# First batch of a dilated sliding-window attention with a SiLU layer behind it: v in two halves, a new order of steps, copies assigned later in the plan, band mask by a scan

## The chip, the cores and the metric

The kernel runs on one core of a Trainium2 chip. It is timed as a whole, in device microseconds; a figure is the median of several executions. The core has five engines with instruction queues of their own: TensorE (PE in the profile; its weight loads are PEld), VectorE (DVE), ScalarE (ACT), GpSimd (POOL) and SyncE (SP). Each engine works through its queue strictly in the order in which the program was written; engines wait for each other through semaphores. Transfers from and to HBM are started by an instruction on POOL, SP or ACT and are then carried out by 16 DMA engines.

## The reference

Attention over 8 batches, 8 heads, 576 positions, head size 64. Heads 0 to 3 look back over 32 positions, heads 4 to 7 over every fourth of the last 128. The result, 4608 tokens by 512, passes through two dense layers.

```python
mask_plain = (rel >= 0) & (rel < window)                       # window 32
mask_dil = (rel >= 0) & (rel < window * dilation) & (rel % dilation == 0)   # dilation 4
masks = np.stack([mask_plain if h < H // 2 else mask_dil for h in range(H)], axis=0)
scores = np.where(masks[None], scale * np.matmul(q, k.transpose(0, 1, 3, 2)), -1000000000.0)
attn = softmax(scores)                                         # over the last axis
x = np.matmul(attn, v).transpose(0, 2, 1, 3).reshape(B * S, H * D)
h = x @ w_in                                                   # 512 x 2048
g = h * (1.0 / (1.0 + np.exp(-h)))
out = g @ w_out                                                # 2048 x 512
```

## The kernel before

Layer 1 and layer 2 work on ten groups of tokens, two of 256 and eight of 512. Layer 1 (`layer1`, from line 849) makes 16 tiles h of 128 columns of the hidden layer by four matmuls each; ScalarE takes the tanh (th), VectorE makes gT of it. Layer 2 (`layer2`) sums 16 matmuls into a y tile; ScalarE copies it to ob and sends it out.

Attention (`attention`) is written per batch as steps with names. TD, TA and TB transpose k and q on PE, and a copy brings them from PSUM to kqD (dilated heads), kP and qP (plain heads). S makes one set of scores and exp gives probs; V copies v of the dilated heads to vd; P and D are the value matmuls of the plain and dilated heads, with a reciprocal and a product on VectorE behind each; XP and XD transpose the result into xA, from which layer 1 reads. Batches 0 to 2 go this way; from batch 3 on k and q are turned by DMA through DRAM (kq_s), two batches ahead.

Batch 0 is special. Its k and q arrive in two parts: rows 0 to 95 (k) and rows 0 to 95 (q) of a tile first, and the remaining 48 rows of both later, as load `k0`. TR and TS transpose that rest. Its masks are added in PSUM, by a matmul of the identity with mask_d or mask_p (line 594), and turned into factors once batch 0 is over (step M, line 638). The masks come from `band`, a 128 x 128 matrix with ones where 0 <= column - row < 32, which POOL makes with a memset and two selects (lines 195 to 200).

The order of everything is made by a planner when the program is built (classes `Step` and `Plan` from line 258 on and the loop at the end). `Plan` keeps a time for PE, times at which ScalarE and VectorE are free, and the times at which PSUM buffers come free; costs in us stand with each `yield`. The loop takes the first step among the next 8 of attention, the next of layer 1 and the next of layer 2 whose inputs are due. Due times of loads are constants: the list `ORDER` is the order of the loads on POOL behind the first ones, `LOAD_US` how long each takes, and `AT_DIL`, `AT_PLAIN`, `AT_VRAW`, `AT_VP` when the first ones land. No time of the planner is seen by the chip: what the program holds is one fixed order per engine.

Where a copy may run on either engine, `best` compares the two engines' free times and gives one. It does so at the moment at which the copy is handed to the planner's queue, with a bias `LEAN` toward ScalarE for batch 0.

POOL's loads use eight semaphores in turn, so that a load is not issued before the load eight places earlier has landed. For v of the plain heads a batch has 24 blocks of 128 rows (4 heads, 6 positions j), 96 rows apart. In batch 0 block 0 of head 0 starts before the tensor and is built from `v_head` (SP, line 190); the other 23 are one load (line 177).

Of the kernel before, what the change touches and what calls it, by code (L numbers as in the profile page):

```python
# [16 lines left out]
def kernel(  # L17
# [18 lines left out]
    MR = M - MA  # L36
    QB = P - W
# [17 lines left out]
    ORDER = "k0 r0 w0a w0b w1 w2 w3 d1 p1 r1 o0 v1 o1 o2 o3".split()  # L55
    LOAD_US = {"w": 2.6, "o": 2.6, "d": 3.7, "p": 3.7, "r": 1.4, "v": 2.6, "k0": 2.0, "r0": 0.9, "w0a": 1.3, "w0b": 1.3}
    AT_W0 = 12.6
# [12 lines left out]
    ident = cpool.tile([P, P], F16, name="ident")  # L70
# [35 lines left out]
    def nat_of(b, key):  # L106
        i = ("k", "q", "rest").index(key)
        return nats[b % 2][:MA, i * RW : (i + 1) * RW].rearrange("p (h r d) -> p h r d", h=H, r=DIL)
# [67 lines left out]
    def issue_vp_first():  # L176
        nc.gpsimd.dma_start(out=vps[0][:, 1:, :D], in_=v_win(QB - W, HN * NB - 1, QB * D))  # L177

    v_head = xRs[2][:, 0, : 2 * D].bitcast(F32)
    for t in vraws[::-1]:  # L180
        nc.vector.memset(t, 0.0)
    nc.vector.memset(v_head[:W], 0.0)
    nc.vector.memset(kqDs[0][:, :, :, 0, MA:], 0.0)
# [6 lines left out]
    nc.sync.dma_start(out=v_head[W:], in_=v[0, 0, :QB])  # L190
# [4 lines left out]
    nc.gpsimd.memset(band, 1.0)  # L195
    for s, base in ((1, 0), (-1, W - 1)):
        nc.gpsimd.affine_select(
            out=band, in_=band, compare_op=ALU.is_ge, fill=0.0, base=base,
            pattern=[[s, P]], channel_multiplier=-s,
        )  # L200
    issue_vp_first()
    nc.vector.tensor_copy(vps[0][:, 0, :D], v_head)
# [4 lines left out]
    nc.vector.memset(mask_p[:W, :2], -BIG)  # L207
    for t in probs:
        c = 2 * 4 * MH
        n = PW + P - c  # L210
        nc.scalar.copy(t[:, c:], vraws[1].rearrange("p a h r d -> p (a h r d)")[:, :n])
# [5 lines left out]
    for what in ORDER:  # L217
        kind, n = what[0], int(what[1])
        if kind == "w":
            f0, f1 = {"": (0, 4), "a": (0, 2), "b": (2, 4)}[what[2:]]  # L220
            cols = slice((4 * n + f0) * P, (4 * n + f1) * P)
            nc.gpsimd.dma_start(out=w_in16[:, :, cols], in_=wi[:, :, cols])
        elif kind == "o":
            nc.gpsimd.dma_start(  # L224
                out=w_out16[:, 4 * n : 4 * n + 4], in_=wo[:, 4 * n : 4 * n + 4]
            )
        elif what == "k0":
            issue_part(k, MA, M, nat_of(0, "rest"), 0, H)
            issue_part(q, MA, M, nat_of(0, "rest")[MR:], 0, H)
        elif what == "r0":  # L230
            issue_vraw(0, (1,))
        elif kind == "d":
            issue_nat(n, HN, H)
        elif kind == "p":
            issue_nat(n, 0, HN)
        elif kind == "r":
            issue_vraw(n)
        else:
            issue_vp(n)
        at += LOAD_US[what] if what in LOAD_US else LOAD_US[kind]  # L240
        AT[what] = at
        if kind == "w":
            for f in range(f0, f1):
                AT_WIN[4 * n + f] = at
# [11 lines left out]
    LEAN = 0.3  # L256
# [6 lines left out]
    class Plan:  # L263
        def __init__(self):
            self.t = 0.0
            self.now = 0.0
            self.free = {"ACT": 0.0, "DVE": 0.0}
            self.heap = []
            self.n = 0
            self.rings = {nm: [] for nm in RINGS}  # L270

        def push(self, step, gen, ready):
            self.now = ready
            try:
                eng, us = next(gen)
            except StopIteration:
                step.done = ready
                return
            heapq.heappush(self.heap, (ready, self.n, step, gen, eng, us))
            self.n += 1  # L280

        def flush(self):
            while self.heap and self.heap[0][0] <= self.t:
# [5 lines left out]
                if eng == "LANDED":  # L289
                    self.push(step, gen, ready)  # L290
                    continue
                end = max(ready, self.free[eng]) + us
                self.free[eng] = end
                self.push(step, gen, end + HOP)
# [36 lines left out]
    AT_DIL = {0: 6.3, 1: AT["d1"], 2: t2 + 7.0}  # L331
    AT_PLAIN = {0: 9.5, 1: AT["p1"], 2: t2 + 7.0}
    AT_VRAW = {0: 10.4, 1: AT["r1"], 2: t2 + 8.6}
    AT_VP = {0: 12.9, 1: AT["v1"], 2: t2 + 11.4}
    AT_CAST = t2 + 18.0
    AT_REST = AT["k0"]
    AT_V1 = AT["r0"]
    AT_WOUT = [AT[f"o{n}"] for n in range(4)]
# [96 lines left out]
    def attention(b):  # L435
# [46 lines left out]
        def best(dve, act):  # L482
            ends = {
                e: max(plan.now, plan.free[e]) + us for e, us in (("DVE", dve), ("ACT", act))
            }
            return ("DVE", dve) if ends["DVE"] + LEAN * (b == 0) <= ends["ACT"] else ("ACT", act)

        def trans_a(ring, hp):
# [6 lines left out]
            for dst, src, us in (  # L495
# [4 lines left out]
                step = best(us, us)  # L500
                yield step
                copy_on(step[0], dst, src.rearrange("p r m -> p m r"))

        def trans_b(ring, hp):
# [3 lines left out]
            step = best(0.47, 0.40)  # L508
            yield step
            qt = qP[:, hp].rearrange("p (m r) -> p m r", r=DIL)  # L510
            copy_on(step[0], qt[:, MR:], tps.rearrange("p r m -> p m r"))

        def trans_d(ring, h):
            tps = small(ring, [P, 2, 3, MA], F16, f"td_{b}_{h}")
            for rp in range(2):
# [5 lines left out]
            step = best(0.37, 0.58)  # L521
            yield step
            copy_on(
                step[0], kqD[:, h].rearrange("p r k m -> p r (k m)"),
# [3 lines left out]
        def trans_d0(ring, h):  # L528
# [6 lines left out]
            step = best(0.34, 0.42)  # L535
            yield step
            copy_on(step[0], kqD[:, h].rearrange("p r k m -> p (r k) m")[:, :, :MA], tps)

        def trans_d1(ring):
            tps = small(ring, [P, 2 * HN, MA], F16, f"td1_{b}")  # L540
            for n in range(2 * HN):
                nc.tensor.transpose(
                    tps[:, n],
                    nat_of(b, "rest")[:, HN + n // 2, n % 2 * 2 : n % 2 * 2 + 2, :], ident[:MA, :MA],
                )
            step = best(0.60, 0.72)
            yield step
            copy_on(
                step[0], kqD.rearrange("p h r k m -> p (h r k) m")[:, :, MA:],
                tps.rearrange("p n (k m) -> p (n k) m", k=2),  # L550
            )

        def trans_a0(ring, hp, nm):
# [7 lines left out]
            step = best(0.47, 0.42)  # L561
            yield step
            dst = (kP[:, hp, W:] if nm == "k" else qP[:, hp])[:, : DIL * MA]
            copy_on(step[0], dst.rearrange("p (m r) -> p m r", r=DIL), tps.rearrange("p r m -> p m r"))

        def trans_a1(ring, hp):
            tps = small(ring, [P, DIL, MA], F16, f"ta1_{b}_{hp}")
            for r in range(DIL):
                for i in range(2):
                    nc.tensor.transpose(  # L570
                        tps[i * D : i * D + D, r], nat_of(b, "rest")[:, 2 * hp + i, r, :],
                        ident[:MA, :MA],
                    )
            for n, dst in enumerate((kP[:, hp, W:], qP[:, hp])):
                step = best(0.27, 0.22)
                yield step
                copy_on(
                    step[0], dst[:, DIL * MA :].rearrange("p (m r) -> p m r", r=DIL),
                    tps[:, :, n * MR : n * MR + MR].rearrange("p r m -> p m r"),
# [46 lines left out]
        def paired(key):  # L626
            step = best(0.335, 0.95)
            yield step
            src = nat_of(b, key)
            copy_on(  # L630
                step[0], pairs[key].rearrange("p g r i d -> p i g r d"),
# [8 lines left out]
        def vd_of(ab):  # L640
            step = best(0.335, 0.95) if pe_path else ("DVE", 0.335)
            yield step
            copy_on(step[0], vd[:, ab, :, :, :D], vraws[b % NV][:, ab])
# [48 lines left out]
        def x_p(ring, j):  # L692
# [6 lines left out]
            step = best(0.17, 0.22)  # L699
            yield step  # L700
            copy_on(step[0], dst, xp)

        def x_d(ring, ab):
# [8 lines left out]
            for hp in range(HP // 2):  # L712
                step = best(0.365, 0.36)
                yield step
                copy_on(step[0], dst[:, hp], xp[:, hp].rearrange("p r m -> p m r"))

        if b == 0:
            order = [
                ("TD", 0), ("TD", 1), ("TD", 2), ("TD", 3), ("S", 3), ("S", 4), ("TA", 0, "k"),
                ("TA", 1, "k"), ("TA", 0, "q"), ("TA", 1, "q"), ("V", 0), ("D", 0, 0), ("D", 0, 1),  # L720
                ("S", 0), ("D", 0, 2), ("S", 1), ("D", 0, 3), ("XD", 0), ("P", 0), ("P", 1), ("P", 2),
                ("XP", 0), ("XP", 1), ("XP", 2), ("TR",), ("TS", 0), ("TS", 1), ("S", 5), ("P", 3),
                ("S", 2), ("V", 1), ("S", 6), ("XP", 3), ("P", 4), ("P", 5), ("D", 1, 0), ("D", 1, 1),
                ("XP", 4), ("XP", 5), ("D", 1, 2), ("D", 1, 3), ("XD", 1), ("M",), ("B",),
# [26 lines left out]
        for key in order:  # L751
# [31 lines left out]
            elif kind == "S":  # L783
                if not pe_path:
                    deps = [turned[b]]
                elif b == 0:
                    deps = [st for key_, st in steps.items() if key_[0] == "TA" and a[0] < 3]
                    deps += [st for key_, st in steps.items() if key_[0] == "TS" and a[0] == 2]
                    deps += [st for key_, st in steps.items() if key_[0] == "TD" and a[0] > 2]
                    deps += [st for key_, st in steps.items() if key_[0] == "TR" and a[0] > 4]  # L790
                elif a[0] < 3:
                    deps = [steps[t, hp] for t in ("TA", "TB") for hp in range(HP // 2)]
                else:
# [3 lines left out]
                    deps + readers.get(base + a[0] - NP, []), ("ACT", "DVE"),  # L797
# [3 lines left out]
            elif kind == "P":  # L801
# [3 lines left out]
                    [at_vp] + [steps["S", u] for u in us], ("DVE",),  # L805
# [131 lines left out]
    while att or l1 or l2:  # L937
# [13 lines left out]
        cands = main + cands if side > 0.5 else cands + main  # L951
        pick, waits = None, []
# [47 lines left out]
```

## Time and profile before

| | us |
|---|---|
| median of 5 runs | 318.32 |
| lowest, highest | 317.58, 321.53 |
| profiled execution, whole | 318.8 |
| its span (first to last instruction) | 317.1 |
| PE busy in the span | 302.9 |
| VectorE busy | 194.7 |
| ScalarE busy | 165.3 |
| POOL busy | 53.5 |

The span is what the instructions cover; the rest of the execution's 318.8 us lies around it. Busy time is the union of an engine's instructions. A matmul's row includes the time that its result takes through the array, so rows of neighbouring matmuls overlap and a busy PE is not always at its peak rate.

How the start goes by in the timeline:

| us | what |
|---|---|
| 5.2 | PE's first transpose (TD), when the first k has landed |
| 6.3 | VectorE scales the band, when POOL has made it |
| 7.8 | first mask matmul of the scores |
| 11.6 | first value matmuls (D) |
| 15.7 | TR, on the rest of k and q |
| 21.2 | first matmuls of layer 1 |
| 32.6 | first transposes of batch 1 |
| 40.1 | first matmuls of layer 2 |
| 58.1 | first transposes of batch 2 |
| 313.2 | last ob |

### The profile page before, as it was taken

Reading aid. Unit: us, or ns where it says so; the run is one execution under the profiler, and the core shown is the slowest. Engines: PE = TensorE matmul, PEld = TensorE weight load, DVE = VectorE, ACT = ScalarE, POOL = GpSimd, SP = SyncE. Lnnn points to the kernel's source line nnn. Section 1 sums busy time; section 2 is a strip of 40 time slices with the busy share of each in tenths; the row PEclk is TensorE's granted clock in tenths of the full one; section 3 lists DMA queues with packets and bytes.
Section 4 is the critical chain, followed back from the end, with each engine's and each line's share of the span. In section 5 each row is a group of like instructions: output and inputs, shape, how many; then the busy total and the mean of one; then the engine's idle time right before and its main releaser. Section 6 shows DMA issues by size and latency. Waiting matters only on the chain.

```text
span 317.1 us, 6091 instructions
## 1 busy us (share of the span) xinstructions
PE 302.9 (96%) x2378; PEld 155.0 (49%) x2378; DVE 194.7 (61%) x489; ACT 165.3 (52%) x306; POOL 53.5 (17%) x85
## 2 busy tenths in 40 slices
PE   2999898999999999999999999999999999999995
PEld 1567774545544544544454444444454444444442
DVE  5448997699788785853777578538773155555000
ACT  7668774477766365444663455446642344555111
POOL 8734814001900005001400050000000000000000
PEclk9999999999999999999999999999999999999999
DMA  7999999998999949998999999990114600000221
GB/s 96 179 203 196 175 201 180 218 174 140 126 199 203 201 99 159 214 189 192 163 180 193 207 158 207 177 219 24 53 54 124 179 2 33 33 33 2 84 81 66
DMA packets 107124, 44.50 MB, mean 140 GB/s; under 512 B 73304, under 2 KB 102488, under 8 KB 107096
## 3 DMA queue, kind: packets, MB, share of 16 engines
q0 software_dynamic: 48848, 19.91, 52.4%
q1 hardware_dynamic: 53064, 14.77, 25.4%
q10 hardware_dynamic: 5184, 9.44, 9.2%
q8 instruction: 18, 0.29, 0.4%
q14 instruction: 10, 0.08, 0.1%
HBM read 39.84 MB, written 18.28 MB: 183 GB/s over the span
## 4 chain that ended last, share of the span: by engine, by line
PE 82%; DMA 12%; POOL 3%; issue 1%; ACT 1%; POOLq 0%
PE y L891 39%; PE h L858 35%; DMA w_out<-in_moe_w_out_dram 5%; DMA nat<-in_q_dram 4%; PE s L606 3%; DMA nat<-in_k_dram 2%; PE av_d L653 2%; PE av_p L653 2%; POOL nat L127 1%; ACT ob L902 1%; POOL w_out L224 1%; POOL vp L177 0%; POOL vp L174 0%; POOL nat L120 0%; PE td L517 0%
## 5 line engine op out<-in xcount | busy, mean ns | idle before, releaser
L891 PE MATMUL y<-w_out,gT 128*128 128x512 f16 x576 | 138.5, 379 | 0.9 <-ACT ob L902 0.9
L869 DVE SCALAR_TENSOR_TENSOR gT<-th,h 128x512 f16<-128x512 f32 (+1 forms) x160 | 98.6, 628 | 60.5 <-ACT th L867 60.1
L867 ACT ACTIVATE th<-h 128x512 f32<-128x512 f32 (+1 forms) x160 | 88.6, 555 | 78.0 <-PE h L858 73.0
L858 PEld LDWEIGHTS <-w_in 128*128 128x128 f16 x640 | 59.0, 98 | 53.6 <-issue 1.1
L891 PEld LDWEIGHTS <-gT 128*128 128x128 f16 x576 | 53.2, 98 | 59.2 <-issue 1.1
L858 PE MATMUL h<-xR,w_in 128*128 128x512 f16 x320 | 77.4, 379 | 0.0
L858 PE MATMUL h<-xA,w_in 128*128 128x512 f16 (+1 forms) x320 | 64.8, 340 | 0.1
L615 ACT ACTIVATE probs<-s 128x768 f16<-128x768 f32 (+2 forms) x47 | 36.6, 779 | 16.5 <-PE s L606 13.7
L902 ACT ACTIVATE ob<-y 128x512 f32<-128x512 f32 x36 | 21.5, 597 | 44.4 <-PE y L891 41.5
L657 DVE TENSOR_TENSOR oD<-av_d,rcps 72x256 f16<-72x256 f32 x64 | 26.9, 421 | 2.2
L653 PEld LDWEIGHTS <-probs 128*128 128x128 f16 x448 | 22.3, 100 | 12.1 <-DVE probs L624 0.6
L657 DVE TENSOR_TENSOR oP<-av_p,rcps 96x256 f16<-96x256 f32 x48 | 20.2, 421 | 1.6
L396 POOL COPY fence<-kqT 128x1 f16<-128x1 f16 x10 | 2.4, 248 | 99.6 <-DMA kqT<-kq_s 99.6
L624 DVE TENSOR_TENSOR probs<-probs,mask_d 128x576 f16<-128x576 f16 (+1 forms) x23 | 11.9, 516 | 6.6 <-ACT probs L615 5.0
L656 DVE RECIPROCAL rcps<-av_p 96x4 f32<-96x4 f32 x48 | 8.3, 174 | 11.2 <-PE av_p L653 11.1
L653 PE MATMUL av_d<-vd,probs 128*128 128x65 f16 x256 | 14.1, 198 | 0.5 <-ACT kP L478 0.4
L656 DVE RECIPROCAL rcps<-av_d 72x4 f32<-72x4 f32 x64 | 11.0, 171 | 5.2 <-PE av_d L653 5.1
L624 DVE TENSOR_TENSOR probs<-probs,mask_p 128x768 f16<-128x768 f16 x21 | 11.6, 554 | 1.8 <-ACT probs L615 1.6
L653 PE MATMUL av_p<-vp,probs 128*128 128x65 f16 x192 | 12.6, 198 | 0.0
L161 POOL DMA_DIRECT2D vraw<-in_v_dram x16 | 11.0, 690 | 6.8 <-DVE rcps L656 3.4
L174 POOL DMA_DIRECT2D vp<-in_v_dram x7 | 10.1, 1445 | 2.1 <-PE s L606 1.8
L480 DVE COPY vd<-vraw 128x1024 f16<-128x1024 f16 x16 | 7.0, 442 | 2.2 <-DMA vraw<-in_v_dram 2.2
(84 smaller groups left out, 141.3 us busy)
## 6 DMA issues: line engine op xcount, KB each, us to landing
out_dram<-ob ACTq DMA_DIRECT2D x36, 256.0 KB, 3.1
kq_s<-in_k_dram POOLq DMA_DIRECT2D x5, 576.0 KB, 11.0
kq_s<-in_q_dram POOLq DMA_DIRECT2D x5, 576.0 KB, 13.6
vp<-in_v_dram POOLq DMA_DIRECT2D x7, 384.0 KB, 9.4
w_out<-in_moe_w_out_dram POOLq DMA_DIRECT2D x4, 512.0 KB, 12.3
vraw<-in_v_dram POOLq DMA_DIRECT2D x8, 224.0 KB, 5.6
w_in<-in_moe_w_in_dram POOLq DMA_DIRECT2D x3, 512.0 KB, 12.8
x_s<-oP SPq DMA_DIRECT2D x10, 144.0 KB, 2.8
```

The source lines that it names most:

```text
L161: nc.gpsimd.dma_start(out=vraw[p0 : p0 + m1 - m0, ab].rearrange("p h r d -> p h (r d)"), in_=src[m0:m1],)
L174: nc.gpsimd.dma_start(out=vps[b % NV][:, :, :D], in_=v_win(b * H * S - W, HN * NB, QB * D))
L615: nc.scalar.activation(p2, both[:, :, :n], AF.Exp, scale=scale)
L624: nc.vector.tensor_tensor(p2, p2, mk, ALU.mult)
L653: nc.tensor.matmul(a[:, i, : D + 1], lhs(i), rhs(i), start=True, stop=True)
L656: nc.vector.reciprocal(rcp[:n], a[:n, :, D : D + 1])
L657: nc.vector.tensor_tensor(o, a[:n, :, :D], rcp[:n, :, None].broadcast_to([n, HN, D]), ALU.mult)
L858: nc.tensor.matmul(h[:, :w], w_in16[:, c, f * P : (f + 1) * P], x_g[:, c], start=(c == 0), stop=(c == HP - 1),)
L867: nc.scalar.activation(th[:, :w], h[:, :w], AF.Tanh, scale=0.5)
L869: nc.vector.scalar_tensor_tensor(gTs[g][:, f, :w], th[:, :w], 1.0, h[:, :w], ALU.add, ALU.mult)
L891: nc.tensor.matmul(y, gTs[g][:, f, tb * P : (tb + 1) * P], w_out16[:, f], start=(f == 0), stop=(f == NFF - 1),)
L902: nc.scalar.activation(ob, y, AF.Copy, scale=0.5)
```

## The change

- v of batch 0 (plain heads): the load of 23 blocks becomes five loads of four blocks (one position j each): j = 1 and 2 where it stood, j = 3 to 5 as a new load `v0` further down in ORDER. Block j = 0 of all four heads comes over SP's `v_head`, which grows from 24 to 96 KB; its copy is issued behind the masks.
- ORDER: the first part of w_in (`w0a`) and `v0` go ahead of `r0`, `w1` ahead of `w0b`, and batch 1's v (`v1`) from behind the first quarter of w_out (`o0`) to behind the last (`o3`). Durations and due times are set anew.
- Copies: a step now yields "ANY" with both costs, and the planner picks the engine when it takes the copy from its queue. LEAN goes from 0.3 to 0.1, and the engines' free times start at 5.7 and 6.6 us instead of 0.
- band: VectorE makes it with one running sum over each row, of the identity less the identity moved by 32 columns (`ident_w`), instead of POOL with a memset and two selects.
- The order of batch 0's steps is another one, S in batch 0 has dependences of its own per set, and the copy of TR is two copies. Steps that need no PE go ahead of the others in the planner's choice.

```diff
-    ORDER = "k0 r0 w0a w0b w1 w2 w3 d1 p1 r1 o0 v1 o1 o2 o3".split()
-    AT_W0 = 12.6
+    ORDER = "k0 w0a v0 r0 w1 w0b w2 w3 d1 p1 r1 o0 o1 o2 o3 v1".split()
+    AT_W0 = 11.4
...
-    ident = cpool.tile([P, P], F16, name="ident")
+    ident_w = cpool.tile([P, W + P], F16, name="ident_w")
+    ident = ident_w[:, W:]
...
-    def issue_vp_first():
-        nc.gpsimd.dma_start(out=vps[0][:, 1:, :D], in_=v_win(QB - W, HN * NB - 1, QB * D))
-
-    v_head = xRs[2][:, 0, : 2 * D].bitcast(F32)
+    def issue_vp_first(j0, j1):
+        for j in range(j0, j1):
+            nc.gpsimd.dma_start(
+                out=vps[0].rearrange("p (i j) c -> p i j c", i=HN)[:, :, j, :D],
+                in_=v_win(QB * j - W, HN),
+            )
+
+    v_head = xRs[2][:, 0, : 2 * HN * D].bitcast(F32).rearrange("p (h d) -> p h d", h=HN)
...
+    nc.vector.memset(ident_w[:, :W], 0.0)
...
-    nc.sync.dma_start(out=v_head[W:], in_=v[0, 0, :QB])
+    nc.sync.dma_start(out=v_head[W:], in_=v[0, :HN, :QB].rearrange("h s d -> s h d"))
...
-    nc.gpsimd.memset(band, 1.0)
-    for s, base in ((1, 0), (-1, W - 1)):
-        nc.gpsimd.affine_select(
-            out=band, in_=band, compare_op=ALU.is_ge, fill=0.0, base=base,
-            pattern=[[s, P]], channel_multiplier=-s,
-        )
-    issue_vp_first()
-    nc.vector.tensor_copy(vps[0][:, 0, :D], v_head)
+    issue_vp_first(1, 3)
+    nc.vector.tensor_tensor_scan(
+        band, ident, ident_w[:, :P], 0.0, ALU.add, ALU.subtract
+    )
...
+    nc.vector.tensor_copy(
+        vps[0].rearrange("p (i j) c -> p i j c", i=HN)[:, :, 0, :D], v_head
+    )
...
-    LEAN = 0.3
+    LEAN = 0.1
...
+                if eng == "ANY":
+                    ends = {e: max(ready, self.free[e]) + n for e, n in us.items()}
+                    eng = min(ends, key=ends.get)
+                    us = us[eng]
...
-            ends = {
-                e: max(plan.now, plan.free[e]) + us for e, us in (("DVE", dve), ("ACT", act))
-            }
-            return ("DVE", dve) if ends["DVE"] + LEAN * (b == 0) <= ends["ACT"] else ("ACT", act)
+            return "ANY", {"DVE": dve + LEAN * (b == 0), "ACT": act}
...
-                ("TD", 0), ("TD", 1), ("TD", 2), ("TD", 3), ("S", 3), ("S", 4), ("TA", 0, "k"),
-                ("TA", 1, "k"), ("TA", 0, "q"), ("TA", 1, "q"), ("V", 0), ("D", 0, 0), ("D", 0, 1),
-                ("S", 0), ("D", 0, 2), ("S", 1), ("D", 0, 3), ("XD", 0), ("P", 0), ("P", 1), ("P", 2),
-                ("XP", 0), ("XP", 1), ("XP", 2), ("TR",), ("TS", 0), ("TS", 1), ("S", 5), ("P", 3),
-                ("S", 2), ("V", 1), ("S", 6), ("XP", 3), ("P", 4), ("P", 5), ("D", 1, 0), ("D", 1, 1),
-                ("XP", 4), ("XP", 5), ("D", 1, 2), ("D", 1, 3), ("XD", 1), ("M",), ("B",),
+                ("V", 0), ("TD", 2), ("TA", 0, "k"), ("TD", 1), ("TD", 3), ("TA", 0, "q"),
+                ("TD", 0), ("TA", 1, "q"), ("S", 4), ("S", 3), ("V", 1), ("TA", 1, "k"),
+                ("D", 0, 0), ("TS", 0), ("S", 0), ("S", 1), ("P", 2), ("XP", 2), ("D", 0, 1),
+                ("D", 0, 3), ("D", 0, 2), ("P", 1), ("XP", 1), ("TR",), ("P", 0), ("S", 5),
+                ("TS", 1), ("S", 2), ("XD", 0), ("XP", 0), ("P", 3), ("XP", 3), ("D", 1, 0),
+                ("P", 4), ("XP", 4), ("P", 5), ("S", 6), ("D", 1, 3), ("D", 1, 1), ("D", 1, 2),
+                ("XD", 1), ("XP", 5), ("M",), ("B",),
...
+        cands = [x for x in cands if not x[1][1].pe] + [x for x in cands if x[1][1].pe]
```

What this makes of the queues, read from the two built programs. On POOL, behind the first four loads of k and q, the order is: identity, v of the dilated heads (first half), v j = 1, j = 2, the rest of k and q, w0a, v j = 3, 4, 5, the second half of the dilated v, w1, w0b, w2, w3, batch 1's k, q and dilated v, the four quarters of w_out, batch 1's v, batch 2's loads. On PE the first h tile is the step behind S 5 and S 2, where before it stood behind S 5 and S 6; batch 1's P steps, which before began ahead of the second quarter of w_out's matmuls, begin behind all four quarters of the first y tile and half of the second. Of batch 1's copies, two of the four of TD and three of TA's go from VectorE to ScalarE, and TB's two and the two of the first XD from ScalarE to VectorE.

## The prediction

> **What bounds the kernel now.** I read the page's busy shares and chain first, then PE's waits, then PE's busy time by stretch, then the timeline of the first 58 us.
>
> ```profile
> PE 302.9 (96%) x2378; PEld 155.0 (49%) x2378; DVE 194.7 (61%) x489; ACT 165.3 (52%) x306; POOL 53.5 (17%) x85
> ...
> PE 82%; DMA 12%; POOL 3%; issue 1%; ACT 1%; POOLq 0%
> ```
>
> PE is the bound of the span, and the chain is PE but for 12% DMA. The stretches show where PE is not full (columns: stretch, its length, then busy time and instruction count of PE, PEld, DVE, ACT, POOL):
>
> ```profile
> 5.20:10.00 4.80, 3.81 (x44) 2.38 (x46) 2.01 (x5) 2.99 (x8) 4.66 (x9) 1.00 1.39 154
> 10.00:15.00 5.00, 4.62 (x70) 3.01 (x67) 2.90 (x9) 3.05 (x8) 3.40 (x5) 1.00 1.79 181
> 15.00:20.00 5.00, 4.24 (x61) 3.10 (x59) 1.87 (x7) 3.50 (x9) 2.68 (x5) 1.00 1.36 203
> ...
> 35.00:40.00 5.00, 3.99 (x58) 3.00 (x57) 4.99 (x14) 3.61 (x12) 3.26 (x5) 1.00 1.79 175
> ...
> 45.00:50.40 5.40, 4.86 (x65) 3.14 (x63) 4.95 (x18) 4.36 (x11) 2.19 (x2) 1.00 1.46 197
> 50.40:58.10 7.70, 6.77 (x61) 3.53 (x60) 4.03 (x15) 2.70 (x7) 1.72 (x3) 1.00 1.82 186
> 58.10:313.00 254.90, 254.90 (x1801) 121.10 (x1799) 154.30 (x358) 125.82 (x211) 23.23 (x37) 1.00 0.76 133
> ```
>
> From 58.1 us on PE has no idle time. So only what brings PE earlier to the point that it reaches at 58.1, the first transposes of batch 2 (line 517), can shorten the span. Before that point PE idles 5.2 us for the first load, which the change leaves alone, and about 5.0 us more (length minus busy, all stretches between). In 35 to 40 VectorE is full (4.99 of 5.00) while ScalarE has 1.4 us free. PE's waits name the causes (total us, times, longest):
>
> ```profile
> PE xp L695 <- DVE oP L657: 1.0, 3, 0.5
> PE ta L492 <- DVE gT L869: 1.0, 2, 0.8
> PE y L891 <- ACT ob L902: 0.9, 2, 0.4
> ```
>
> There is a second, hidden loss: until 23.4 us matmuls run at half rate. In the timeline the same four 128x256 matmuls take
>
> ```profile
> 22.62 1.04 PE L858 MATMUL h<-xA,w_in 128*128 128x256 f16 x4
> ...
> 24.36 0.61 PE L858 MATMUL h<-xA,w_in 128*128 128x256 f16 x4
> ```
>
> although the granted clock stands at 1.00 in every stretch. And there is a limit that is not PE's: the loads. The chain up to 58 us is
>
> ```profile
> 34.50 15.93 DMA w_out<-in_moe_w_out_dram
> 50.42 0.04 issue
> 50.47 1.04 PE y L891 x4
> ```
>
> The last quarter of w_out lands at 50.42 and PE takes it 0.05 us later. POOL's loads land one after another; before that quarter stands batch 1's v (issued 31.60, 10.3 us to landing: 41.9).
>
> **The change, part by part.**
>
> *Loads.* Up to this last quarter the same loads are issued, in another order: batch 1's v goes from behind the first quarter of w_out to behind the last. So in the new kernel batch 1's v is what lands last. Only 3 of 23 blocks leave POOL's queue (block 0 of the other three heads, now in SP's v_head load): 3/23 of the 3.1 us between the landings of the first vraw half (10.6) and of vp (13.7), 0.4 us. Batch 1's v lands at 50.42 - 0.4 = 50.0, w_out's last quarter some 3.5 us ahead of it (in the trace v landed 3.5 after the first quarter, 30.86 + 7.5 = 38.4). v_head grows from 24 to 96 KB; the small one landed in 1.7 us, by 2.5, ahead of POOL's first landing at 5.2; I put it at 0, at most 0.3 us on the first transposes.
>
> The v load in five pieces costs POOL about 5 x 0.65 us of issue (a nat load of 384 rows takes 0.67; vp's one issue 1.49), 1.8 us more, less the band's memset and two selects, which end (5.34 to 6.27 in the chain) 0.9 us. POOL has 1.3 us of idle time before its issue at 13.98 and later waits 7.7 us for w_in landings, so this hides. Each issue also waits for the landing of the load eight earlier; five of these eight are now short. With landings at 10.6 (vraw), then two pieces of 4/23 x 3.1 = 0.54 us each, the rest of k and q lands at 10.6 + 1.1 + 1.9 = 13.6 instead of 15.6 (8.35 + 7.2), and w_in's first eighth right after it. There are still some 5 us of transfers queued whenever POOL waits, so I expect no hole.
>
> *Band by a scan.* VectorE's first use of the band waits 2.5 us, until 6.30, for POOL. The identity is ready at 4.74. [...] I take 0.35: band at 5.1, scaled 5.3.
>
> [...]
>
> ```profile
> 6.22 1.49 POOL L177 DMA_DIRECT2D vp<-in_v_dram  x1
> ...
> 6.53 1.24 DVE L204 COPY mask_d<-band 128x432 f16<-128x432 f16 x1
> ```
>
> The copy ends with POOL's issue; its smaller twin beside POOL's next issues takes 0.22. [...] The new kernel has POOL issuing without a pause from 4.7 to 8.6. [...] By the rows (0.22 and 0.30 beside nat issues) they are through at 6.2. PE's transposes end at 7.3, so the sum is 0.3 us gained or 0.
>
> *First batch on PE.* The mask wait (0.27) goes, but next late is q's plain half, at 9.7 (3.49 + 6.2): of the 0.5 us some 0.3 remain at the first value matmuls, which start when vd is copied (10.65 + 0.77, again beside a POOL issue). The wait for the rest of q (0.26) goes. The wait of the first xp for oP (0.51) goes: 16 transposes now stand between, and the td1 copy, 0.80 us on ScalarE, is split over two engines. The two xp waits at 27 to 28 us (0.4) have value matmuls between them. Together 1.4 us up to the dense layer 1.
>
> *Engine chosen when the copy comes up.* This acts while the program is planned; on the chip it is another fixed assignment. In batch 1 two of four kqD copies (0.45 each) and three ta copies (0.54, 0.34, 0.34) move from VectorE to ScalarE, two tb copies (0.49) move back: VectorE sheds about 1.1 us in the stretch where it is full; two xd copies (0.40 each) come to it later, near 43, where it is nearly as full (4.80 of 5.00), so I count no gain there. The 1.0 us of PE idle there should shrink to 0.3. Between 45 and 50 us the value steps that made PE wait are moved behind w_out's last quarter (0.3).
>
> So PE gains 0.3 + 1.1 + 0.7 + 0.3 = 2.4 us before 50. *The order behind that* decides: when the new PE order comes to its first matmul on batch 1's v, it holds against the old order at 50.47 (counted in both programs) 12 more y matmuls at 0.216 (2.6) and one more score set (0.3), less six value steps (24 matmuls at 0.03) and four xp pairs (8 at 0.05): 1.8 us more work. PE gets there at 50.47 + 1.8 - 2.4 = 49.9. v lands at 50.0: the load sets the time, by a little.
>
> From there to batch 2's first transposes the new order has 24 y matmuls at 0.216 (48 take 10.36), 40 value matmuls at 0.03 (8 take 0.24) and 12 xp at 0.05: 5.2 + 1.2 + 0.6 = 7.0, and I allow 0.3 for waits (before, two ob waits cost 0.9; the y tiles now change slots). It arrives at 57.3. By then it has done 12 more y matmuls than the old order at 58.1 (2.6 us), less the eight xd transposes that come later (0.3). Gain: 58.1 + 2.3 - 57.3 = **3.1 us** at most, 2.8 with v at 50.3. Batch 2's q lands at 36.63 + 19.4 = 56.0, so it doesn't bind. Later batches turn k and q by DMA: turned from 65.5 to 74.3 and first used at 83.4, a slack of 9 us, so the gain is kept to the end.
>
> The profiled execution took 318.8 (span 317.1); 318.8 - 2.8 = 316.0. The median of the runs is 0.5 lower: 315.5; with 0.1 for v_head I say 315.6.
>
> [...]
>
> **The rivals.**
> *Late on PE* (0.27): the clock is released a window later, or the first batch's in-order queues stall in new places. PE comes to v at 51.3 and the gain is 1.5: 316.8. For it: 1.4 us of the gains are small waits that the next one can swallow. Against: idle ScalarE.
> *Faster yet* (0.18): v lands by 49 and PE is there; the next limit is batch 2's q at 56.0, a gain of up to 4.4: 314.
> *Slower* (0.10): the load queue starves. With eight slots, five of them 131 KB pieces, POOL stops behind a wait (also for engines: it waited 3.1 us for a VectorE read) and no transfers are queued. Batch 1's v stands last, and behind it, in PE's order, everything. Zero gain is passed when v lands at 53.1, 1% when at 56.3; two holes of 3 us would do: 322. Against: in the trace the transfers run on while POOL waits 2 us at a time.
> *The forecast* (0.45): v at 50.0 to 50.5, 314.9 to 316.2.
>
> **How the numbers follow.** 1% is 3.2 us, about what a measurement of this kernel tells from no change; below 315.1 counts as faster. That line runs through the forecast case: 0.20 of its 0.45 and the 0.18 beyond it give 0.38 faster; the rest of it, the late case and 0.01 of the slow one 0.53 same; 0.09 slower. The range leaves out the starved case and the best end: 313.4 to 318.6, which also holds the unknown scan and lock (0.3 each).
>
> **What would show it.** Right: the first mask matmul right after the transposes; batch 1's P matmuls starting at the landing of v near 50; batch 2's transposes at 57 to 57.5; no PE idle after. Wrong: v landing past 51, ScalarE ending PE's waits in 30 to 40, the first 0.109 us spacing of h later than 24, or a gain visible at 58 us and gone by 100.

## The result and the profile after

| | before | after |
|---|---|---|
| median, us (runs) | 318.91 (51) | 317.25 (30) |
| lowest, highest | 315.92, 322.28 | 314.94, 320.15 |
| profiled execution, whole | 318.8 | 316.7 |
| its span | 317.1 | 314.9 |

The ratio after to before is 0.995, 95% interval 0.9935 to 0.9966: the change saves 1.66 us by the medians, 1.1 to 2.1 us by the interval, and 2.2 us between the two profiled spans. The forecast was 2.8. The profiled execution of the changed kernel is 0.55 us faster than its median, so leads read from profiles come out a little larger than the medians give.

The page of the changed kernel, its busy shares and the engines of its chain:

```profile
PE 302.0 (96%) x2378; PEld 154.1 (49%) x2378; DVE 199.3 (63%) x499; ACT 163.2 (52%) x300; POOL 54.2 (17%) x86
...
PE 86%; DVE 7%; ACT 3%; DMA 1%; issue 1%; ACTq 0%; POOL 0%; POOLq 0%
```

The 12% of DMA in the old chain, which was the road through the last quarter of w_out, is 1% now; in its place stand PE and 10% of VectorE and ScalarE. The stretches of the changed kernel (length, then busy time and count of PE, PEld, DVE, ACT, POOL; then the granted clock):

```profile
5.20:10.00 4.80, 4.09 (x50) 2.63 (x52) 2.38 (x9) 2.65 (x7) 4.32 (x7) 1.00 1.47 164
...
15.00:20.00 5.00, 5.00 (x66) 3.36 (x63) 3.02 (x10) 3.51 (x11) 3.21 (x5) 1.00 1.36 200
20.00:25.00 5.00, 4.06 (x62) 2.90 (x57) 3.38 (x13) 2.67 (x7) 1.92 (x3) 1.00 1.26 205
...
35.00:40.00 5.00, 4.72 (x65) 3.46 (x64) 5.00 (x15) 4.25 (x13) 2.36 (x4) 1.00 1.24 207
...
45.00:50.40 5.40, 5.40 (x56) 2.83 (x54) 3.96 (x10) 3.01 (x8) 2.21 (x2) 1.00 1.79 179
50.40:58.10 7.70, 7.70 (x89) 4.75 (x87) 6.70 (x26) 2.40 (x6) 0.93 (x2) 1.00 1.71 204
58.10:313.00 254.90, 251.82 (x1769) 119.16 (x1767) 154.68 (x356) 126.26 (x211) 22.54 (x37) 1.00 0.75 133
```

From 45 to 58 us PE is full, where it idled 0.54 and 0.93 us before; in 35 to 40 it idles 0.28 instead of 1.01, with VectorE as full as it was. But the last line is no longer full: it has 254.90 less 251.82, that is 3.08 us of idle time. Some 2.0 us of these are the earlier end (PE's last matmul ends at 311.0), the rest is new. The waits of PE behind 58 us, a list that was empty for the kernel before, now read (total us, times, longest)

```profile
PE h L862 <- DVE gT L873: 0.5, 2, 0.3
PE av_p L656 <- DVE probs L629: 0.3, 1, 0.3
```

**The lead at equal work.** Since the order of the instructions changed, clock times of the two traces can't be subtracted line by line. I add up PE's work in the order of each program, every matmul at its usual spacing (h and y of 512 columns 0.216 us, value matmuls 0.030, transposes 0.03 to 0.05), and compare when each trace has done the same amount. The lead over the kernel before, in us; the first column is the time in the trace of before. From the last h or y matmul ahead of a set of scores to the first matmul behind it 0.55 to 0.61 us pass (medians of the kernel before, behind 60 us), against 0.216 between two h or y matmuls. By an estimate from this a set costs PE about 0.2 us more than the sum counts, so a figure moves by up to 0.3 where one order has such a set earlier than the other:

| before is at | after | undo_v1 | undo_any | undo_order | undo_scan | tail_before | head_after | late_x9 | vd_act |
|---|---|---|---|---|---|---|---|---|---|
| 28.3 | 0.8 | 1.9 | 3.3 | 2.3 | -0.5 | 2.9 | 2.3 | 1.1 | 2.5 |
| 61.8 | 4.1 | 2.5 | 3.5 | 4.1 | 2.8 | 3.4 | 2.2 | 4.2 | 4.1 |
| 85.2 | 4.0 | 2.5 | 3.4 | 4.0 | 2.7 | 3.3 | 2.2 | 4.1 | 4.0 |
| 104.2 | 3.0 | 1.8 | 3.1 | 3.0 | 1.8 | 2.3 | 2.2 | 3.2 | 3.2 |
| 176.8 | 3.1 | 0.5 | 3.1 | 3.0 | 1.9 | 1.4 | 2.2 | 2.4 | 3.2 |
| 218.5 | 1.8 | 0.5 | -1.9 | 0.0 | -2.0 | 1.4 | 2.2 | 2.6 | 2.5 |
| 311.4 | 2.2 | 0.5 | -3.4 | -0.3 | -1.7 | 1.4 | 2.2 | 2.4 | 2.5 |

The column "after" has the riddle: 4.1 us are won by 62 us, more than the 2.8 to 3.1 forecast, and 1.9 are lost again by the end. All edits below are to the changed kernel. Each column is one profiled execution; the medians follow with each run, and their ratios are to executions of the kernel before taken with that run.

### The profile page after: what moved, and what is told of

It reads as the page before. It is cut to its first block, busy times and chain, and to the rows that moved or that the text cites. A ratio compares the mean times of both kernels' runs of the same rounds, so it can differ in the third digit from the quotient of the medians.

```text
span 314.9 us, 6098 instructions
## 1 busy us (share of the span) xinstructions
PE 302.0 (96%) x2378; PEld 154.1 (49%) x2378; DVE 199.3 (63%) x499; ACT 163.2 (52%) x300; POOL 54.2 (17%) x86
## 4 chain that ended last, share of the span: by engine, by line
PE 86%; DVE 7%; ACT 3%; DMA 1%; issue 1%; ACTq 0%; POOL 0%; POOLq 0%
PE y L895 37%; PE h L862 35%; PE s L611 4%; DVE gT L873 3%; PE av_d L656 3%; PE av_p L656 2%; DMA nat<-in_q_dram 1%; PE s L599 1%; DVE oP L660 1%; ACT th L871 1%; DVE probs L629 1%; DVE vd L494 1%; ACT ob L906 1%; ACT probs L620 1%; ACT xA L492 1%
## 5 line engine op out<-in xcount | busy, mean ns | idle before, releaser
L620 ACT ACTIVATE probs<-s 128x768 f16<-128x768 f32 (+2 forms) x46 | 35.8, 779 | 15.0 <-PE s L611 14.1
L656 PE MATMUL av_d<-vd,probs 128*128 128x65 f16 x256 | 14.9, 196 | 0.8 <-ACT xA L492 0.4
L494 DVE COPY vd<-vraw 128x1024 f16<-128x1024 f16 x16 | 8.1, 512 | 0.3 <-DMA vraw<-in_v_dram 0.3
```

The lines of the kernel that those rows point to most:

```text
L494: nc.vector.tensor_copy(dst, src)
L620: nc.scalar.activation(p2, both[:, :, :n], AF.Exp, scale=scale)
L656: nc.tensor.matmul(a[:, i, : D + 1], lhs(i), rhs(i), start=True, stop=True)
```

## Experiments

**undo_v1: batch 1's v back in its old place among the loads.**

```diff
-    ORDER = "k0 w0a v0 r0 w1 w0b w2 w3 d1 p1 r1 o0 o1 o2 o3 v1".split()
+    ORDER = "k0 w0a v0 r0 w1 w0b w2 w3 d1 p1 r1 o0 v1 o1 o2 o3".split()
```

> Only batch 1's v goes back behind the first quarter of w_out. Theory A (each load in front of its first use sets the time up to 58 us): w_out's last quarter lands at about 49 instead of 45, batch 1's P steps come earlier again; the lead at equal work at 58 us falls from 4.1 to 2 to 2.5 us, and the whole to 318.0 or more. Theory B (the lead up to 58 us comes from copies and order, the place of v does nothing by itself): lead at 58 us 3.5 to 4.1, whole 317.0 to 317.6.

318.62 us, ratio 1.0005 (0.9969 to 1.0042). The lead at 62 us is 2.5 instead of 4.1, as Theory A had it: the place of this one load, with the plan that follows from it, carries 1.6 us of the gain. By the ratios it carries all of it (1.0005 against 0.995); the two intervals, this one and that of the change, do not overlap, but only just. The lead also shrinks later, to 0.5, though PE is less far ahead here. PE's order is another one from 42 us on, and that turned out to be the point.

**undo_any: the engine of a copy chosen at hand-over, as before.**

```diff
-            return "ANY", {"DVE": dve + LEAN * (b == 0), "ACT": act}
+            ends = {
+                e: max(plan.now, plan.free[e]) + us for e, us in (("DVE", dve), ("ACT", act))
+            }
+            lean = 0.3 * (b == 0)
+            return ("DVE", dve) if ends["DVE"] + lean <= ends["ACT"] else ("ACT", act)
```

> The engine of a copy is chosen when it is handed over, with the old bias of 0.3, all else as changed. Theory A (VectorE is the bound between 25 and 50 us, and the late choice frees it): the PE idle time near 35 to 40 us comes back, lead at 58 us about 1.3 us smaller, whole about 318.3. Theory B (the order and the loads do it): lead at 58 us within 0.5 of 4.1, whole 317.0 to 317.7.

323.48 us, ratio 1.0138 (1.008 to 1.0195). At 62 us 0.6 us of lead is missing, near what Theory B allows, so in this profile the choice is worth about that much where it acts. The total was in neither forecast: 5.0 us are lost between 177 and 218 us and 1.5 behind that. The largest loss in this kernel's timeline:

```profile
212.28 1.03 PE L866 MATMUL h<-xR,w_in 128*128 128x512 f16 x4
215.43 1.89 PE L866 MATMUL h<-xR,w_in 128*128 128x512 f16 x4 [2.12 <-DMA xR<-x_s]
```

SP's queue ahead of it:

```profile
204.27 6.58 SPq L154 DMA_TRANSPOSE nat<-kq_s  x2
210.99 1.84 SPq L433 DMA_TRANSPOSE xR<-x_s  x1
```

Layer 1 of the later batches reads x that a DMA has transposed (xR), and in SP's queue that transpose stands behind the turns of k and q of a later batch. PE waits 2.12 us for it, and then four h matmuls take 1.89 instead of 1.03, and four more after them as long: half rate again, for 3.4 us. Here the granted clock shows it (third number from the end, 0.50):

```profile
215.40:218.80 3.40, 3.37 (x8) 1.19 (x9) 0.69 (x1) 0.60 (x1) 0.00 (x0) 0.50 0.59 118
```

Eight matmuls at some 0.42 instead of 0.216 us cost another 1.6. Wait and half rate together are 3.7 of the 5.0.

**undo_order: batch 0's steps in their old order** (the list of steps of the diff, the removed lines put back).

> Batch 0's list of steps as before, all else as changed. Theory A (the searched order takes out 1.4 us of PE waits before layer 1): PE has done 8 us worth of matmuls 1 us later than with the change (22.7 against 21.7), whole 317.8 to 318.5. Theory B (the lead won in batch 0 is lost again at 22 to 25 us, as the trace of the changed kernel shows it falling from 1.25 to 0.1, so the order is worth nothing): whole 317.0 to 317.6, or less.

317.59 us, ratio 0.996 (0.9927 to 0.9992); the lead at 62 us is 4.1, the same as with the searched order: Theory B. Nothing measurable hangs on that order. This profile also has one wait of 1.9 us for xR, at 178 us, which takes its lead.

**undo_scan: band made by POOL with a memset and two selects, ahead of v's first two pieces.**

```diff
-    nc.vector.memset(ident_w[:, :W], 0.0)
...
+    nc.gpsimd.memset(band, 1.0)
+    for s, base in ((1, 0), (-1, W - 1)):
+        nc.gpsimd.affine_select(
...
-    nc.vector.tensor_tensor_scan(
-        band, ident, ident_w[:, :P], 0.0, ALU.add, ALU.subtract
-    )
```

> The band is made by POOL as before, ahead of v j = 1 and 2. Theory A (q's plain half at 9.7 us is the next limit, so the scan is worth 0.3 us at most): first mask matmul 0.4 to 0.5 us later, first value matmuls at most 0.3 later, whole 317.2 to 317.7. Theory B (the 0.9 us on POOL delay v and the rest of k and q, which the first batch now needs early): PE waits at v j = 1 or at the rest of k, whole 318 or more.

317.46 us, ratio 0.9969 (0.9935 to 1.0003). The lead at 62 us is 1.3 less, which looks like the price of the scan. It is not safe to read it so, because this profile differs in one more thing. The first h of layer 1 in the timelines of three kernels: changed, tail_before (which is the changed kernel up to 118 us) and undo_scan; for the kernel before, the prediction shows the same rows at 22.62 and 24.36:

```profile
20.12 1.02 PE L862 MATMUL h<-xA,w_in 128*128 128x256 f16 x4
21.67 0.61 PE L862 MATMUL h<-xA,w_in 128*128 128x256 f16 x4
```

```profile
18.44 0.61 PE L862 MATMUL h<-xA,w_in 128*128 128x256 f16 x4
```

```profile
22.43 1.04 PE L864 MATMUL h<-xA,w_in 128*128 128x256 f16 x4
24.66 0.60 PE L864 MATMUL h<-xA,w_in 128*128 128x256 f16 x4 [0.46 <-DVE rcps L661]
```

Matmuls go at half rate until some moment: four h matmuls of 256 columns take 1.02 to 1.04 us ahead of it and 0.60 or 0.61 behind it. The trace keeps the moment, as the first entry of its record of the granted clock: 20.99 in the changed kernel's profile, 23.70 in undo_scan's, but 14.77 in tail_before's. The same program up to 118 us got its full rate 6.2 us sooner in one execution than in another. At half the rate for 2.7 us more, undo_scan lost an estimated 1.35 us to this alone, as much as its lead is short. The medians give no price for the scan: 0.2 us, inside both intervals, in the range of Theory A.

This run also serves as a second look at the change: its PE order is the changed kernel's from the first matmul to the last. The lead falls between 85 and 104 us here too, by 0.9, though it is smaller, and behind 179 us PE waits 3.1 us for xR.

These four left two explanations of the later loss. Theory A: PE, running ahead, uses up the slack of the transfers for x. Theory R: the newly planned order of the later steps costs, whatever the lead. The next four runs go on from there.

**tail_before: from about 118 us on, the planner's picks are forced into the sequence that the kernel before has.** FORCED holds one letter for each pick (x: next of layer 1, y: next of layer 2, a digit: which attention step).

```diff
+    FIRST = 259
+    made = 0
...
+        if FIRST <= made < FIRST + len(FORCED):
+            c = FORCED[made - FIRST]
+            q_, it, lim = {"x": (l1, l1[:1], 1.3), "y": (l2, l2[:1], 9.0)}.get(c) or (att, att[int(c) :][:1], 1.0)
...
+            plan.start(it[1])
+            continue
```

> The changed kernel, but from about 118 us of the plan on its picks are made in the sequence of the kernel before. Theory A (running ahead uses up the slack of the transfers for x): the 4 us that PE leads by at 60 us are given back whatever the order, here at an x group of batches 3 and later (a PE wait of 1 to 3 us for the transposed x) or by stalls as large; ratio to the kernel before 0.995 to 1.0. Theory R (the newly planned order is what costs): without that order nothing is lost after 118 us, the lead of about 3.1 us there stays to the end; ratio 0.990, and no PE wait over 0.3 us after 118 us.

317.57 us, ratio 0.9953 (0.9929 to 0.9977). At the splice PE waits 0.6 us for a score buffer; behind it the lead stays at 1.4 to 1.6 to the end. Ahead of it, where the order is still the changed one, it falls from 3.4 to 2.4. The total lies in Theory A's range (0.995 to 1.0; R had 0.990), but without the x wait or the later losses that A named: what R said of the stretch behind the splice holds, apart from the 0.6 us at the splice itself.

**head_after: the changed kernel's picks up to about 40 us, v in its old place, then before's sequence.**

```diff
-    ORDER = "k0 w0a v0 r0 w1 w0b w2 w3 d1 p1 r1 o0 o1 o2 o3 v1".split()
+    ORDER = "k0 w0a v0 r0 w1 w0b w2 w3 d1 p1 r1 o0 v1 o1 o2 o3".split()
...
+    FIRST = 0
```

> The changed kernel's picks up to about 40 us, batch 1's v loaded in its old place among the output weights, then the sequence of picks of the kernel before. Theory A: a lead of 2.3 to 2.5 us at 60 us as in the run that undid the load alone; less of it lost than in the changed kernel because PE runs less far ahead, the rest lost at x of batches 3 and later or in PE waits before 100 us: ratio 0.995 to 1.0. Theory R (the newly planned order costs): the lead of about 2.4 us stays to the end, ratio 0.9925.

317.37 us, ratio 0.996 (0.9926 to 0.9994). By the total this is Theory A's range (0.995 to 1.0) and not R's 0.9925; the profiled execution, at 316.71, is 0.66 faster than the median. Its profile is the clearest of all: the lead is 2.2 at 62 us and 2.2 at the end, and PE has no wait at all behind 58 us. The last stretch of its table:

```profile
58.10:313.00 254.90, 252.90 (x1772) 119.53 (x1770) 153.37 (x358) 125.32 (x208) 23.14 (x37) 1.00 0.75 133
```

The 2.0 us that are missing are the earlier end. Beside it stands undo_v1, with the same load in the same place and a lead of 2.5 at 62 us, but the planner's own order behind it. Its waits behind 58 us:

```profile
PE h L862 <- DMA xR<-x_s: 0.7, 1, 0.7
PE h L862 <- DVE gT L873: 0.4, 1, 0.4
PE av_d L656 <- DVE probs L629: 0.3, 1, 0.3
```

It loses 2.0 us where head_after loses none. At a lead of 2.2 to 2.5 us it is the order that costs, not the running ahead: Theory R, as far as these two profiles go. The largest of the three waits is one for x, which another execution may not have. Whether the lead of 4.1 would survive in before's sequence too was not run.

**late_x9: the planner takes 9.0 instead of 6.0 us for the transpose of x**, so that layer 1's groups of batches 3 and later come later in PE's order.

```diff
-        yield "DMA", 6.0
+        yield "DMA", 9.0
```

> The changed kernel, whose plan takes 9.0 instead of 6.0 us from the issue of an x transpose to its landing, so that the first-layer groups of batches 3 and later stand later in PE's order. Theory A: no PE wait for transposed x in the profile, less spread of the times, the lead of about 3 us at 110 us kept to within 0.7 at the end; ratio 0.991 to 0.993, below the 0.995 of the changed kernel. Theory R: the order is changed again without a cause, so 0.995 or above. If the fill work that stands in for the groups runs out, PE waits at the end instead and the ratio is 0.997 or more.

317.44 us, ratio 0.9955 (0.9919 to 0.999): no better than the changed kernel, as Theory R had it, which speaks against x waits as what holds its typical execution back. Its profile keeps 2.4 us; the stalls between 84 and 93 us are there again.

**vd_act: the copies of the dilated v of batches 3 and later on ScalarE.**

```diff
-            eng = yield best(0.335, 0.95) if pe_path else ("DVE", 0.335)
+            eng = yield best(0.335, 0.95) if pe_path else ("ACT", 0.95)
```

> The changed kernel, but the copies of the dilated v of batches 3 and later run on ScalarE and are planned there at 0.95 us. Theory P (the loss at 180 us is a VectorE copy held up beside POOL's descriptor writing): no copy of 1.4 us, no wait of PE for probs at 180 us, lead at 190 us 0.5 to 0.7 larger than in the changed kernel; ratio 0.993. Theory A: PE is then further ahead at the next x group and loses it there; ratio 0.994 to 0.997, with a PE wait for transposed x of 0.5 us or more in the profile.

The reason for this run is a row of the changed kernel's timeline, a copy that takes 0.41 elsewhere:

```profile
178.56 1.52 POOL L177 DMA_DIRECT2D vp<-in_v_dram  x1
...
178.95 1.36 DVE L494 COPY vd<-vraw 128x1024 f16<-128x1024 f16 x1
...
180.82 0.30 PE L656 MATMUL av_p<-vp,probs 128*128 128x65 f16 x4 [0.34 <-DVE probs L629]
```

It ends 0.23 us behind POOL's issue, and the probs behind it in VectorE's queue come late for PE. With the copy on ScalarE, the same place reads

```profile
177.87 1.04 ACT L492 COPY vd<-vraw 128x1024 f16<-128x1024 f16 x1
177.95 1.43 POOL L177 DMA_DIRECT2D vp<-in_v_dram  x1
```

and PE's value matmuls there wait for nothing. The edit does not isolate the copy: the plan changes with it, PE's order is another one from 91 us on, and four h matmuls now stand between that set of scores and the next value matmuls. The lead at 218.5 is 0.7 larger, as Theory P had it, and 0.3 larger at the end: PE stands 0.35 us at each of two places, behind y matmuls at 193.7 and 225.7 us, both times for gT. The time is not better: 317.62 us, ratio 0.9953 (0.9911 to 0.9996), of 8 executions three near 321. PE had no wait for transposed x in the profile, so Theory A's mechanism failed for this run, though the ratio is in its range and not at P's 0.993.

## Why the prediction missed

*The loads: right, with a spread that the forecast lacked.* Batch 1's v was put at 50.0; it landed at 48.8 in the profile of the change, and between 48.5 and 50.2 in the six experiments that keep this order of loads. "The load sets the time, by a little" holds in some executions and not in others. In tail_before, v landed at 50.23:

```profile
50.27 0.66 PE L656 MATMUL av_p<-vp,probs 128*128 128x65 f16 x16 [1.50 <-DMA vp<-in_v_dram]
```

In the changed kernel's profile, PE comes to the same matmuls at 49.6, 0.8 behind the load. The rest of k and q landed at 13.61 (forecast 13.6), q's plain half at 9.74 (9.7).

*The band and the masks: right.* No run shows the 0.35 us that the forecast takes for the scan; in the profile of the change it took 0.42. The band was there at 5.10 and scaled at 5.33 (forecast 5.1, 5.3). The mask copies were put at 6.2 by the rows of before; in the changed kernel's timeline:

```profile
4.68 0.42 DVE L204 TENSOR_TENSOR_SCAN band<-ident_w 128x128 f16<-128x128 f16 x1 [0.83 <-POOL ident_w masks.py:199]
5.13 0.20 DVE L207 TENSOR_SCALAR band<-band 128x128 f16<-128x128 f16 x1
5.36 0.27 DVE L208 COPY mask_d<-band 128x432 f16<-128x432 f16 x1
5.55 0.51 DVE L209 COPY mask_d<-band 128x288 f16<-128x288 f16 x1
5.98 0.24 DVE L210 COPY mask_p<-band 128x576 f16<-128x576 f16 x1
```

They end at 6.22. The "or 0" of the forecast's first gain and the "lock" of its range assume that a copy has to wait out an issue of POOL's; that was the author's assumption, and the runs show it of single copies only. Of the three mask copies beside POOL's issues two took 0.27 and 0.24; the third took 0.51, where before's took 0.22, and ends 0.06 behind an issue of 0.76. Of the 16 copies of 128x1024 in this profile one, at 179 us, took 1.36 beside an issue of 1.52, 0.95 more than the usual 0.41, and two others some 0.3 more.

*The clock: not in the sum, and little of the time hangs on it.* By the trace's record, full rate came at 23.86 in the kernel before (read as 23.4 from its matmuls) and at 20.99 in the profile of the change, 2.9 earlier. But late_x9, tail_before and vd_act, which run the same program up to 91 us at least, had it at 12.80, 14.77 and 15.16, so one profile of each kernel does not tell what the change did to it. The "window" by which *Late on PE* has the clock released later was the author's assumption; no run shows what a release waits for. What the traces show is the time after it: where the granted clock changes again, it does so whole multiples of 3.413 us after the release (in late_x9 10.24 and 13.65 us after it, in undo_any 201.38 and 204.80). Why the changed kernel's profile was released later than those three is not shown.

It decides little of the time, because the gain is capped further on. At 28 us tail_before led by 2.9, late_x9 (at half rate again from 23.04 to 26.45) by 1.1 and the changed kernel by 0.8; at 62 us it was 3.4, 4.2 and 4.1. The early one waited for v.

*The gain at 58 us: mis-sized by 0.3 to 1.1.* The sum gave 2.8 to 3.1; the kernels that share the changed start (after, late_x9, vd_act, tail_before) show 3.4 to 4.2. In the profile of the change, PE went from v's first matmul to batch 2's transposes in 6.95 us (49.59 to 56.54), where I had 7.0 and 0.3 for waits that did not come, and it started 0.4 earlier than v's forecast landing.

*"From 58.1 us on PE has no idle time", so "the gain is kept to the end": the step that failed.* It was read off the trace of before, in which that stretch is 254.90 of 254.90. But that trace is of one order, and the planner, started from other times, makes another one from 40 us on. The table of leads has it: 1.8 us lost behind 85 us in the changed kernel, 1.7 and 1.5 in late_x9 and vd_act, none in head_after. The loss was put at nothing and is 1.9 us from 62 us on; that the total came within 1.2 us of the forecast is partly luck, since the gain ahead of it was larger than forecast by 1.0 to 1.3. One of the places can be read step by step. In the changed kernel:

```profile
82.82 1.89 PE L862 MATMUL h<-xA,w_in 128*128 128x512 f16 x8
...
84.58 0.69 DVE L873 SCALAR_TENSOR_TENSOR gT<-th,h 128x512 f16<-128x512 f32 x1 [0.52 <-ACT th L871]
84.65 0.35 PE L611 MATMUL s<-nat 64*128 64x96 f16 x8
...
85.32 1.89 PE L862 MATMUL h<-xA,w_in 128*128 128x512 f16 x8 [0.32 <-DVE gT L873]
```

Two tiles of h, a score set, and two tiles of h again. The kernel before, at the same steps of attention:

```profile
84.86 1.03 PE L858 MATMUL h<-xA,w_in 128*128 128x512 f16 x4
85.82 0.35 PE L606 MATMUL s<-nat 64*128 64x96 f16 x8
86.10 1.04 PE L891 MATMUL y<-w_out,gT 128*128 128x512 f16 x4
86.97 1.89 PE L858 MATMUL h<-xA,w_in 128*128 128x512 f16 x8
```

One tile of h, the scores, four y matmuls, and then the two tiles. The y matmuls need nothing that VectorE is only just making, and give it the time to read the old h tile out of PSUM. Without them PE stands until gT is made: 0.5 us from the last score matmul to the next h, where 0.13 is usual. The same stall is at 85.18 in late_x9, 86.01 in tail_before, 85.26 in vd_act and 86.58 in undo_scan, at leads from 2.7 to 4.1: it belongs to the order, not to an execution and not to how far PE is ahead. The next, at 92 to 94 us, returns in all but vd_act, whose order is another one by then.

Counted from the usual spacing, PE stands at five places of the changed kernel's profile behind 80 us: at 84.8 and 92.6 (0.4 us each), 180.3 (0.4), 182.6 (0.3) and 214.6 (0.2), together 1.7 of the 1.9. Four are h matmuls that wait for a gT; at 180.3 value matmuls wait for probs. The first two and the last return in undo_scan, which has the same PE order; the other two are of this execution.

*What remains.* The 0.4 us at 180 us go to the held-up copy by the changed kernel's own rows: ScalarE's exp is done at 179.70 and VectorE's product takes 0.54, so with a copy of 0.41 us probs would have been ready by an estimated 180.24, and PE is through with its scores at about 180.4. vd_act agrees and does not prove it. Waits for x of 0.7 to 3.1 us came in the profiles of four variants and not in that of the changed kernel. The prediction weighed the turns of k and q, with 9 us of slack, and not the transposes of x that stand behind them in SP's queue. undo_scan's profile is of the slowest of its ten executions, 320.49 against a median of 317.46, and its wait for x is 3.1; as its PE order is that of the changed kernel, such waits may make the slowest executions of that one too (five of 30 are above 319), but none of these was profiled. The profiles' 2.2 lies just above the medians' interval of 1.1 to 2.1, being a single pair of executions. Of the rivals, *Faster yet* named the size at 62 us (up to 4.4), with v by 49; *Late on PE*, at 316.8, came nearest to the end, by another road.

Nothing that was run beats the changed kernel by more than the intervals allow. The kernel that these runs point to, its start up to 60 us with the old sequence behind it, was not run.

## What to carry to other kernels

A stretch without idle time proves that this order has none there; if a planner makes the order, an earlier start gives another order, and the gain must be looked for at the end, not at the point where it was made. Compare traces at equal work of the bounding engine: the lead then shows where time is won and where it is lost again, and a second profile of the same instructions, as undo_scan gave it here, shows which of it is chance. Where the plan puts several tiles of one kind in a row, look at which buffer the second waits for, and which other work could stand between.

## What the runs showed of the hardware

- The time at which TensorE goes to full rate differs by 8 us between executions of the same instructions (12.80, 14.77, 15.16 and 20.99 us in late_x9, tail_before, vd_act and the changed kernel). The granted clock of the profile's rows reads 1.00 ahead of it too (the changed kernel's 15 to 20 us), and the record's first entry is at the release; that first stretch has to be read from the length of known matmuls (1.02 and 0.61 us for the same four).
- The clock changed at whole multiples of 3.413 us after the release (3 and 4 in late_x9, 59 and 60 in undo_any), and both falls to half rate lasted one such step, 3.4 us: the row of undo_any has a granted clock of 0.50, and in late_x9 ten h matmuls of 256 columns took 2.29 us where twelve take 1.47 at full rate.
- A wait of 2.12 us was followed by half rate in undo_any, waits of 1.88 and 3.11 us (undo_order, undo_scan) were not: four h matmuls behind them took 1.02. Counted in steps of 3.413 us from the release, the idle time of PE tells them apart. The steps of undo_any and late_x9 ahead of the two falls held 2.07 and 2.06 us of it. The waits of 1.88 and 3.11 us lie across the end of a step, with at most 1.60 and 2.01 us of idle PE in one. In the ten profiles, between the release and the last matmul, no step but the two ahead of the falls held more than 2.01. Two falls are few to make a rule of.
- A VectorE copy of 128x1024 took 1.36 instead of 0.41 beside a DMA issue of POOL of 1.52 us. The copies of this size held up by 0.25 us or more in the two main profiles, four in all, end 0.22 to 0.25 us behind the end of such an issue. Others run beside one unhindered: before's at 47.55 took 0.42 within an issue of 1.52 from 47.50.
